# Cosine attention and a highway layer on one core: the order on each engine is handed from a manual schedule to the tile scheduler

## The chip, the cores and the metric

The kernel runs on one core of one Trainium2 chip. A core has five engines that each take instructions from a queue of their own: TensorE (PE, matrix products; its weight loads are listed apart as PEld), VectorE (DVE), ScalarE (ACT), GpSimd (POOL) and SyncE (SP), which here issues nearly all DMA transfers. [...] The metric is the device time of one execution in microseconds (us); lower is better.

## The reference

The work is a cosine-similarity attention over 8 batches with 12 heads of 448 positions and 64 dimensions, and behind it a highway layer on the 3584 x 768 result:

```python
q_n = q / (norm(q) + 1e-6);  k_n = k / (norm(k) + 1e-6)
scores = q_n @ k_n.T / tau                     # tau = 0.1
attn = exp(scores - max); attn /= sum(attn)
x = (attn @ v), heads side by side              # 3584 x 768
H = max(x @ w_h, 0);  T = sigmoid(x @ w_t + b_t)
out = T * H + (1 - T) * x
```

## The kernel before

**Tiles.** Four heads of one batch make a quad; there are 24 quads, three for each batch. The 448 positions are cut into a main part of 384 and a tail of 64; with its tails packed in pairs a quad is seven chunk-steps (`ci` 0 to 6). A step is one pair of score products on PE into a PSUM tile `sp` of two banks (line 258 for `ci` 0, line 266 for the others), one exponential on ACT of 128 x 896 into the tile `e` (line 279), and a share of the products of `e` with v (`av_slot`, line 295) into a PSUM tile `u` (main) or `ut` (tail). When a `u` is complete, DVE takes the reciprocal of the row sums (`rd`, line 319) and scales into `x` (line 321); a `ut` likewise (lines 343 and 344) into `xtail`.

**Preparing a quad.** `load_qk` brings q and k (line 91, and two short transfers each at line 100) into one of six `raw` buffers. ACT squares q (`sqq`, line 141), POOL squares k (`sqk`, line 147), DVE sums the squares (line 151) and makes the inverse root with integer and multiply steps (`rsqrt`, lines 158 to 170). POOL scales q and k (`qn` and `kn`, lines 182 to 211), and two transposing DMAs on SP (`turn`, lines 220 and 226) make `qT` and `kT`. DVE casts v (`vm` and `vt`, lines 236 and 243). The weights come in twelve transfers (line 123) through three `wst` buffers, and DVE casts each (line 127); the bias comes as `bt_raw` (line 464) and is halved on DVE into `bth` (line 465).

**The highway layer.** When the three quads of a batch are done, `ffn_items` queues its three row tiles of 128 (and for every second batch one tile of tails). A tile is six transposes on PE into `xp` (line 363), one copy on DVE into `xT` (line 365), and four groups of six products `pt` (line 381), two with w_t, which also get a bias product (line 394) and a tanh on ACT (`tt`, line 398), and two with w_h, which DVE turns into `hm` (line 386), `th` (line 407) and `o` (line 411). The result `o` goes out by SP (lines 419 and 425). A pool of two PSUM buffers holds `xp` and `pt`, another of two holds `u` and `ut`, a third of two holds `sp`.

**What sets the order.** The end of the kernel function emits everything step by step: the score product of the next step, the exponential of this one, a share of the av products, a ration of highway items (`RATE` 4.6 a step, taken from the queue `ffq`), and the preparing work that `prep` lists for this step. Line 68, `ctx.enter_context(tc.manual_schedule())`, binds this: inside the region each engine issues its instructions in the order in which they were emitted. The semaphores, and the buffers that the pools hand out, are worked out from that order.

Of the kernel before, what the change touches and what calls it, by code (L numbers as in the profile page):

```python
# [20 lines left out]
def kernel(  # L21
# [43 lines left out]
    u_ps = pool("u_ps", 2, space=PS)  # L65
    p_ps = pool("p_ps", 2, space=PS)

    ctx.enter_context(tc.manual_schedule())

    ident = const.tile([128, 128], FP16)  # L70
    w_h_f = const.tile([128, CC, DM], FP16)
# [536 lines left out]
```

## Time and profile before

| | |
|---|---|
| median of 2 runs | 468.95 us (466.25 and 471.65) |
| the profiled execution | 467.99 us, of which the span is 466.2 |
| busy: PE, DVE, ACT, POOL | 295.5, 275.6, 189.8, 156.2 us |
| mean granted TensorE clock | 0.87 |
| DMA moved | 61.03 MB, 131 GB/s |

No engine is busy for more than 63% of the span, so the idle time of PE, the busiest, and what ended it, is the thing to look at. The span has three parts that are read apart: the start, up to the first score product of quad 4 at 105.28 us, in which inputs and weights come in; the middle, from there to the first transposes of the last batch's highway tiles at 431.14 us, in which attention and highway layer run side by side; and the end, where four highway tiles are left.

### The profile page before, as it was taken

To read this page: it belongs to the slowest core of one execution; us is meant where nothing else is said; L and a number is where in the kernel's file an instruction comes from. 1 tells how busy PE (TensorE), PEld (TensorE's weight loads), DVE (VectorE), ACT (ScalarE), POOL (GpSimd) and SP (SyncE) were. 2 spreads that over 40 slices of the span, in tenths; PEclk is the share of its full clock that TensorE was granted. 3 is DMA by queue.
4 is the path that set the end of the run, shared out by engine and by line. 5 is a ranking of instruction groups with operands and counts; after the bars stand their busy time and mean duration, and the time that the engine had idled before them with its cause. 6 is when DMAs were issued, how large, how long until landed. Compare 5 with 4: busy or idle time off the path is not lost.

```text
span 466.2 us, 7225 instructions
## 1 busy us (share of the span) xinstructions
PE 295.5 (63%) x2768; PEld 157.3 (34%) x2768; DVE 275.6 (59%) x589; ACT 189.8 (41%) x249; POOL 156.2 (34%) x196
## 2 busy tenths in 40 slices
PE   0114051475784687775787688785588668888673
PEld 0002030232441344442343344343244334445342
DVE  3902996636762654685356777765456555555553
ACT  1224052343462554444345455552455235664110
POOL 2541742634253065136054436342530830000000
PEclk9999997668996988895758999989588879999989
DMA  9669599842935475553855294469353332200102
GB/s 243 154 149 268 146 268 269 191 105 67 250 47 141 128 190 126 134 101 90 221 124 141 82 251 101 104 150 219 95 97 77 77 77 65 48 36 35 67 34 67
DMA packets 111460, 61.03 MB, mean 131 GB/s; under 512 B 69441, under 2 KB 106305, under 8 KB 111426
## 3 DMA queue, kind: packets, MB, share of 16 engines
q1 hardware_dynamic: 110610, 60.12, 51.7%
q10 hardware_dynamic: 816, 0.46, 0.3%
q8 instruction: 21, 0.34, 0.3%
q14 instruction: 13, 0.11, 0.1%
HBM read 37.75 MB, written 11.01 MB: 105 GB/s over the span
## 4 chain that ended last, share of the span: by engine, by line
PE 37%; DVE 32%; SPq 9%; DMA 8%; POOL 5%; ACT 4%; issue 4%; DVEq 0%; ACTq 0%; POOLq 0%
PE pt L381 21%; PE u L295 7%; PE sp L266 6%; DVE o L411 6%; DMA raw<-in_q_dram 6%; DVE th L407 5%; DVE hm L386 4%; DVE n L151 4%; SPq L100 3%; DVE xT L365 3%; DVE x L321 3%; SPq L226 2%; ACT sqq L141 2%; ACT e L279 2%; PE pt L394 2%
## 5 line engine op out<-in xcount | busy, mean ns | idle before, releaser
L279 ACT ACTIVATE e<-sp 128x896 f16<-128x896 f32 x168 | 146.1, 917 | 45.3 <-PE sp L266 30.1
L381 PE MATMUL pt<-w_t_f,xT 128*128 128x384 f16 x336 | 86.2, 376 | 66.2 <-DVE xT L365 66.2
L266 PE MATMUL sp<-qT,kT 64*128 64x448 f16 x288 | 61.8, 424 | 58.4 <-ACT e L279 58.2
L381 PEld LDWEIGHTS <-xT 128*128 128x128 f16 x672 | 61.8, 106 | 108.9 <-DVE xT L365 71.1
L398 ACT ACTIVATE tt<-pt 128x384 f16<-128x384 f32 x56 | 27.5, 491 | 144.4 <-PE pt L394 144.4
L147 POOL TENSOR_TENSOR sqk<-raw 128x896 f16<-128x896 f32 x24 | 41.7, 1737 | 133.1 <-DMA raw<-in_k_dram 114.4
L295 PEld LDWEIGHTS <-e 128*128 128x128 f16 x1536 | 66.5, 106 | 53.3 <-issue 49.1
L381 PE MATMUL pt<-w_h_f,xT 128*128 128x384 f16 x336 | 80.3, 354 | 0.0
L182 POOL TENSOR_TENSOR qn<-raw,rs 128x384 f16<-128x384 f32 x46 | 41.0, 911 | 81.0 <-DVE rs L170 41.8
L295 PE MATMUL u<-vm,e 128*128 128x65 f16 x864 | 56.8, 209 | 17.2 <-DVE x L321 17.2
L319 DVE RECIPROCAL rd<-u 128x6 f32<-128x6 f32 x48 | 9.3, 193 | 84.2 <-PE u L295 84.2
L141 ACT ACTIVATE sqq<-raw 128x896 f16<-128x896 f32 x24 | 22.8, 948 | 73.4 <-DMA raw<-in_q_dram 65.8
L266 PEld LDWEIGHTS <-kT 64*128 64x128 f16 x288 | 15.9, 95 | 107.1 <-issue 102.4
L295 PE MATMUL u<-vt,e 128*128 128x65 f16 x288 | 48.8, 207 | 0.0
L386 DVE SCALAR_TENSOR_TENSOR hm<-pt,x 128x384 f16<-128x384 f32 x48 | 26.6, 554 | 37.3 <-PE pt L381 36.8
L202 POOL TENSOR_TENSOR kn<-raw,rs 128x384 f16<-128x384 f32 x48 | 42.7, 910 | 4.7 <-DVE rs L170 4.7
L407 DVE SCALAR_TENSOR_TENSOR th<-tt,hm 128x384 f16<-128x384 f16 x56 | 33.4, 596 | 5.8
L411 DVE SCALAR_TENSOR_TENSOR o<-x,th 128x384 f32<-128x384 f16 x48 | 30.0, 624 | 1.7
L151 DVE TENSOR_REDUCE n<-sqq 128x14 f32<-128x896 f16 x24 | 25.8, 1075 | 5.7 <-ACT sqq L141 5.6
L321 DVE SCALAR_TENSOR_TENSOR x<-u,rd 128x384 f16<-128x384 f32 x48 | 26.8, 557 | 1.6
L258 PE MATMUL sp<-qT,kT 128*128 128x448 f16 x48 | 15.0, 398 | 20.0 <-DMA kT<-kn 20.0
L151 DVE TENSOR_REDUCE n<-sqk 128x14 f32<-128x896 f16 x24 | 25.8, 1075 | 0.0
(43 smaller groups left out, 245.4 us busy)
## 6 DMA issues: line engine op xcount, KB each, us to landing
raw<-in_q_dram SPq DMA_DIRECT2D x24, 384.0 KB, 4.1
vr<-in_v_dram SPq DMA_DIRECT2D x8, 1152.0 KB, 7.2
out_dram<-o SPq DMA_DIRECT2D x24, 384.0 KB, 2.5
raw<-in_k_dram SPq DMA_DIRECT2D x23, 384.0 KB, 4.1
wst<-in_moe_w_h_dram SPq DMA_DIRECT2D x6, 384.0 KB, 5.4
wst<-in_moe_w_t_dram SPq DMA_DIRECT2D x6, 384.0 KB, 5.0
raw<-in_q_dram SPq DMA_DIRECT2D x48, 32.0 KB, 3.6
vtr<-in_v_dram SPq DMA_DIRECT2D x16, 96.0 KB, 6.7
```

The lines of the kernel that those rows point to most:

```text
L147: nc.gpsimd.tensor_mul(sq[:, :, :], rk, rk)
L151: nc.vector.reduce_sum(n2[:, qd, 14 * t : 14 * t + 14], st.pop((("sqq", "sqk")[t], Q))[:, :, :], axis=AX.X)
L182: eng.tensor_mul(qn[:, 4 * i : 4 * i + 3, :].rearrange("p j (h d) -> p h j d", h=2), raw[:, 6 * i : 6 * i + 6].rearrange("p (h j) d -> p h ...
L202: eng.tensor_mul(kn[:, 3 * i : 3 * i + 3, :].rearrange("p j (h d) -> p h j d", h=2), raw[:, g : g + 6].rearrange("p (h j) d -> p h j d", h=2),
L266: nc.tensor.matmul(sp[:, h, 0:S], lhsT=kT[hp, ci - 1, :], rhs=qT[hp, s * S : (s + 1) * S], start=True, stop=True,)
L279: nc.scalar.activation(st["e", Q][:, o : o + 2 * S].rearrange("p (a n) -> p a n", a=2), st.pop(("sp", g))[:, :, 0:S], AF.Exp, scale=inv_tau,)
L295: nc.tensor.matmul(u[:, slot, :], lhsT=e[:, o : o + 128], rhs=rhs, start=(kc == 0), stop=(kc == 3),)
L321: nc.vector.scalar_tensor_tensor(out=x[:, :, h0 : h0 + 2, :], in0=u[:, :, 0:D].rearrange("p (t h) d -> p t h d", h=2), scalar=0.0, in1=rd[ ...
L381: nc.tensor.matmul(loc["pt"][:, :], lhsT=loc["xT"][:, cc, :], rhs=w_f[:, cc, ms], start=(cc == 0), stop=(cc == CC - 1 and w_i == 0),)
L386: nc.vector.scalar_tensor_tensor(out=loc["hm"][:, ms], in0=loc["pt"][:, :], scalar=0.0, in1=xf[:, ms], op0=ALU.max, op1=ALU.subtract,)
L407: nc.vector.scalar_tensor_tensor(out=th[:, :], in0=loc["tt"][:, ms], scalar=1.0, in1=loc["hm"][:, ms], op0=ALU.add, op1=ALU.mult,)
L411: nc.vector.scalar_tensor_tensor(out=loc["o"][:, ms], in0=xf[:, ms], scalar=2.0, in1=th[:, :], op0=ALU.mult, op1=ALU.add,)
```

## The change

Line 68 is taken out. There is no other edit: every instruction, operand, buffer count and the emission are the same.

```diff
-    ctx.enter_context(tc.manual_schedule())
+
```

Without the region the tile scheduler sets the order while the program is built. It walks along a clock of its own with an estimated duration for every instruction and transfer. Whenever an engine comes free on that clock, it is given, of the instructions whose inputs and buffers are ready by then, the one that was emitted first. So the emission order stays as the priority, and an instruction is passed by later ones only while the scheduler holds it to be waiting. The order that comes out is fixed in the program; on the chip each engine still takes its queue from the front.

All 7225 instructions are there in both kernels. In the last tenth of PE's queue nothing changes place. On SP three transfers pass a neighbour before quad 14, and more behind it. Three places matter below. Numbers at the end of a name tell one buffer's uses apart; the numbers of the changed kernel are lower by two for the same thing (`u_592` before is `u_590` now).

The first place is DVE's queue in the start, around the bias (`bth`) and the first weight casts. In the kernel before, they stand after quad 1's v casts and ahead of the sums of quad 2 (`sqq_271`, `sqk_273`), with quad 0's first scaling (`x`) further behind:

```order
L236 CAST vm1_115<-vr_127 128x12x64
L243 CAST vt1_118<-vtr_128 64x2x64 x2
L465 TENSOR_SCALAR bth_108<-bt_raw_109 1x768
L151 TENSOR_REDUCE n2_172<-sqq_271 128x14
L151 TENSOR_REDUCE n2_172<-sqk_273 128x14
L158 TENSOR_SCALAR rs_173<-n2_172 128x28
```

In the changed kernel, DVE's queue has them here, right behind the scaling of quad 1's second half (`u_590`):

```order
L319 RECIPROCAL rd_631<-u_590 128x6
L236 CAST vm1_113<-vr_241 128x12x64
L321 SCALAR_TENSOR_TENSOR x_359<-u_590,rd_631 128x3x128
L243 CAST vt0_115<-vtr_242 64x2x64
L243 CAST vt1_116<-vtr_242 64x2x64 x2
L465 TENSOR_SCALAR bth_106<-bt_raw_107 1x768
L127 CAST w_h_f_104<-wst_248 128x768
L127 CAST w_h_f_104<-wst_250 128x768
```

The bias and the casts moved back past the sums of quads 2 to 4 and past all scalings of quads 0 and 1. The casts free the `wst` buffers, and SP's queue, which did not change there, has the fourth weight transfer ahead of quad 2's transposes.

The second place is one highway tile of the middle (`xp_1684` before, `xp_1682` now; weight loads and repeats left out). On PE before, the first product group follows the transposes at once, and the next step's scores come behind its first two products:

```order
L295 MATMUL ut_1669<-vt1_118,e_1493 128x65
L363 MATMUL xp_1684<-ident_105,x_863 128x128
L381 MATMUL pt_1696<-w_t_f_107,xT_1691 128x384
L266 MATMUL sp_1699<-qT_1377,kT_1419 128x448
L295 MATMUL ut_1669<-vm1_115,e_1493 128x65
```

On PE in the changed kernel, two score products, eight av products and one half of the next scores stand between:

```order
L363 MATMUL xp_1682<-ident_103,x_861 128x128
L266 MATMUL sp_1697<-qT_1375,kT_1417 128x448
L295 MATMUL ut_1667<-vm1_113,e_1491 128x65
L295 MATMUL ut_1667<-vt1_116,e_1491 128x65
L266 MATMUL sp_1723<-qT_1375,kT_1417 128x448
L381 MATMUL pt_1694<-w_t_f_105,xT_1689 128x384
```

On DVE, the copy that these products wait for (`xT`) stood before behind the tile ahead's `hm`, `th` and `o`:

```order
L386 SCALAR_TENSOR_TENSOR hm_1515<-pt_1627,x_863 128x384
L407 SCALAR_TENSOR_TENSOR th_1680<-tt_1516,hm_1515 128x384
L411 SCALAR_TENSOR_TENSOR o_1517<-x_863,th_1680 128x384
L365 COPY xT_1691<-xp_1684 128x768
L343 RECIPROCAL rdt_1712<-ut_1669 64x4
```

and now stands on DVE right behind `hm`:

```order
L386 SCALAR_TENSOR_TENSOR hm_1513<-pt_1625,x_861 128x384
L365 COPY xT_1689<-xp_1682 128x768
L407 SCALAR_TENSOR_TENSOR th_1678<-tt_1514,hm_1513 128x384
L343 RECIPROCAL rdt_1710<-ut_1667 64x4
L411 SCALAR_TENSOR_TENSOR o_1515<-x_861,th_1678 128x384
```

So the copy moved ahead of two operations on DVE, and its reader moved back past a step of attention on PE. Counted over all 28 tiles, 21 had nothing between their transposes and their first product group before; in the changed kernel only the four tiles of the end have nothing between. There the copy still moves ahead of `th` and `o`.

The third place is ACT's queue in quads 2 and 3, and in it the squares of a later quad's q. Before, the squares of quad 7 (`raw_540`) stand behind the third exponential of quad 2 (`e_569`), and those of quad 8 (`raw_697`) behind the first of quad 3 (`e_722`):

```order
L141 ACTIVATE sqq_636<-raw_540 128x896
L279 ACTIVATE e_569<-sp_617 128x896
L279 ACTIVATE e_569<-sp_643 128x896
L279 ACTIVATE e_569<-sp_653 128x896
L279 ACTIVATE e_569<-sp_675 128x896
L279 ACTIVATE e_722<-sp_705 128x896
L141 ACTIVATE sqq_735<-raw_697 128x896
```

In the changed kernel, the squares of quad 7 stand on ACT behind the fourth exponential of quad 3 (`e_720`), and those of quad 8 behind the first of quad 4 (`e_915`):

```order
L279 ACTIVATE e_720<-sp_756 128x896
L141 ACTIVATE sqq_634<-raw_538 128x896
L279 ACTIVATE e_720<-sp_802 128x896
L279 ACTIVATE e_720<-sp_815 128x896
L279 ACTIVATE e_720<-sp_845 128x896
L398 ACTIVATE tt_785<-pt_787 128x384
L398 ACTIVATE tt_785<-pt_837 128x384
L279 ACTIVATE e_915<-sp_881 128x896
L141 ACTIVATE sqq_733<-raw_695 128x896
```

They moved back by eight and by seven exponentials. The squares of quad 6 moved from behind the third exponential of quad 1 to behind its last; those of quad 3 from behind quad 0's third exponential to behind its fourth. Those of quads 10 and 11 moved back by seven, those of quads 12 to 17 by none to four, and from quad 18 on they moved forward, with their loads on SP.

## The prediction

> **What bounds the kernel now.** I read the page first, for an engine that could be the bound by its work alone, then the busy time of PE in the three parts of the span, then what PE waited for in each part, and last the stretches that carry a wait.
>
> ```profile
> span 466.2 us, 7225 instructions
> ...
> PE 295.5 (63%) x2768; PEld 157.3 (34%) x2768; DVE 275.6 (59%) x589; ACT 189.8 (41%) x249; POOL 156.2 (34%) x196
> ...
> L279 ACT ACTIVATE e<-sp 128x896 f16<-128x896 f32 x168 | 146.1, 917 | 45.3 <-PE sp L266 30.1
> ...
> L319 DVE RECIPROCAL rd<-u 128x6 f32<-128x6 f32 x48 | 9.3, 193 | 84.2 <-PE u L295 84.2
> ```
>
> No engine is full. The windows of PE (length, busy time and count, granted clock, DMA share, GB/s) put the start, the middle and the end side by side:
>
> ```profile
> 0.00:105.28 105.28, 32.42 (x299) 0.89 0.79 199
> 105.28:431.14 325.86, 242.21 (x2343) 0.86 0.48 117
> 431.14:466.20 35.06, 20.88 (x130) 0.92 0.16 56
> ```
>
> The waits of PE alone (total, times, longest), first of the start, then of the middle, then of the end:
>
> ```profile
> PE sp L266 <- ACT e L279: 34.7, 8, 9.9
> PE sp L258 <- DMA kT<-kn: 20.0, 1, 20.0
> PE u L295 <- DVE x L321: 17.2, 1, 17.2
> ...
> PE pt L381 <- DVE xT L365: 57.5, 23, 5.1
> PE sp L266 <- ACT e L279: 23.6, 12, 6.6
> PE xp L363 <- DVE x L321: 2.3, 3, 1.5
> ...
> PE pt L381 <- DVE xT L365: 8.1, 4, 2.0
> ```
>
> In the middle the account closes: 242.2 busy and 57.5 + 23.6 + 2.3 = 83.4 waiting make 325.6 of 325.9 us. So the middle is PE's work plus three waits, 20 quads at 16.3 us each. The largest wait is for the copy `xT`, 2.5 us each time. The busy time holds a loss of its own, which single quads show (columns: length; PE, PEld, DVE, ACT and POOL busy; clock; DMA):
>
> ```profile
> 136.50:156.40 19.90, 12.09 (x107) 6.22 (x106) 8.36 (x18) 7.06 (x10) 4.01 (x5) 0.74 0.53 135
> 274.60:286.50 11.90, 10.26 (x120) 5.83 (x119) 8.90 (x17) 8.36 (x12) 5.76 (x7) 1.00 0.63 149
> 389.70:402.00 12.30, 10.26 (x121) 5.84 (x119) 6.59 (x17) 7.58 (x11) 0.00 (x0) 1.00 0.31 74
> ```
>
> The same amount of products takes 12.1 us at a clock of 0.74 and 10.26 at 1.00. The middle's mean is 12.1 a quad, so at most 20 x 1.85 = 37 us of it is slow clock. The two fast quads, at 11.9 and 12.3 us, show how short a quad gets when the waits stay away.
>
> **The start, term A.** The timeline, in order of time (start, length, engine, line, what; in brackets the idle time before and what ended it):
>
> ```profile
> 3.58 2.82 SPq L114 DMA_DIRECT2D vtr<-in_v_dram  x2
> 11.80 0.19 DVE L169 TENSOR_TENSOR ta<-ta,rs 128x28 f32<-128x28 f32 x1
> 12.03 0.19 DVE L170 SCALAR_TENSOR_TENSOR rs<-ta,rs 128x28 f32<-128x28 f32 x1
> 12.91 1.66 DVE L182 TENSOR_TENSOR qn<-raw,rs 128x384 f16<-128x384 f32 x2
> 20.03 0.93 PE L258 MATMUL sp<-qT,kT 128*128 128x448 f16 x2 [20.03 <-DMA kT<-kn]
> 32.96 0.95 ACT L141 ACTIVATE sqq<-raw 128x896 f16<-128x896 f32 x1 [8.59 <-DMA raw<-in_q_dram]
> 36.63 0.92 ACT L279 ACTIVATE e<-sp 128x896 f16<-128x896 f32 x1 [0.30 <-PE sp L266]
> 38.14 0.92 ACT L279 ACTIVATE e<-sp 128x896 f16<-128x896 f32 x1 [0.60 <-PE sp L258]
> 42.95 0.55 DVE L465 TENSOR_SCALAR bth<-bt_raw 1x768 f16<-1x768 f32 x1 [18.88 <-DMA bt_raw<-in_moe_b_t_dram]
> 53.75 0.55 DVE L127 CAST w_h_f<-wst 128x768 f16<-128x768 f32 x1
> 62.61 0.95 ACT L141 ACTIVATE sqq<-raw 128x896 f16<-128x896 f32 x1 [15.52 <-DMA raw<-in_q_dram]
> 66.82 0.94 PE L258 MATMUL sp<-qT,kT 128*128 128x448 f16 x2
> 79.72 0.95 ACT L141 ACTIVATE sqq<-raw 128x896 f16<-128x896 f32 x1 [8.49 <-DMA raw<-in_q_dram]
> 81.90 0.35 SPq L123 DMA_DIRECT2D wst<-in_moe_w_t_dram  x1
> 83.92 0.94 PE L258 MATMUL sp<-qT,kT 128*128 128x448 f16 x2
> 87.55 1.76 DVE L127 CAST w_t_f<-wst 128x768 f16<-128x768 f32 x2
> 105.28 0.54 PE L258 MATMUL sp<-qT,kT 128*128 128x448 f16 x2
> ...
> DMA to landing us min/median/max: 5.8/6.7/9.3
> ```
>
> The last row is of `vtr`. The first edit is a loss: DVE now has the v casts ahead of and among quad 0's inverse root. The second tail transfer is issued near 5.0 and lands 5.8 to 9.3 later, at 10.8 to 14.3, with 3.6 us still to come: eight root steps and six tail casts of 0.22 us (the distance of the rows at 11.80 and 12.03) and a cast of 0.55 like the one at 53.75. So `qn`, begun at 12.91, begins at 14.4 to 17.9, and the first product comes 1.5 to 5 us later; I take 4, at 24.
>
> Quad 3's squares still stand in front of an exponential of quad 0, and their load is still behind quad 1's transposes on SP, so that wait ends some 3 us later than at 32.96 too, and the exponentials go on at about 37. Ten are then left in quads 0 and 1. The rows at 36.63 and 38.14 give 1.51 us for a step, so quad 1 is through at 37 + 15 = 52 and its last `x` at about 55. Three stalls that held quad 1 before are gone: `bth` no longer stands in front, the squares of quad 6 (15.52 us of waiting) come behind its last exponential, and `x` of quad 0 doesn't wait 17.2 us.
>
> This gain is given back at once. The weight casts now stand behind that last `x`, so they begin at 55 instead of 53.75, and SP has the fourth weight transfer, which needs a freed buffer, ahead of quad 2's transposes. Quad 2 therefore starts at 68, where it was 66.82; PE idles 13 us. What stays is behind it. Quad 2 ran into the squares of quad 7 (8.49 us); these now come in quad 3, so its seven steps take 10.6 us and quad 3 starts at 78.5, not 83.92. Quad 3 waits for the last w_t weights: their transfer was issued at 81.90 and cast by 89.3, and stands now behind the last `x` of quad 2 (about 80) and one more cast, so it comes 0 to 2 us later, and PE finishes the two product groups that need it and starts quad 4 at about 92. Term A is 92 - 105.28 = -13. Its bounds are -16 (quad 3 at 1.51 us a step from 78.5, weights no later) and +3 (the weights later by a transfer of about 5 us at each of three places where SP waits for a cast).
>
> **The middle, term B.** The copy `xT`: its DVE place is priced by the end of the run, where nothing else is between.
>
> ```profile
> 432.05 0.56 DVE L407 SCALAR_TENSOR_TENSOR th<-tt,hm 128x384 f16<-128x384 f16 x1
> 432.64 0.56 DVE L411 SCALAR_TENSOR_TENSOR o<-x,th 128x384 f32<-128x384 f16 x1
> 433.12 0.55 DVE L365 COPY xT<-xp 128x768 f16<-128x768 f16 x1
> 440.50 1.15 PE L381 MATMUL pt<-w_t_f,xT 128*128 128x384 f16 x6 [2.04 <-DVE xT L365]
> 447.28 2.10 PE L381 MATMUL pt<-w_t_f,xT 128*128 128x384 f16 x6 [2.04 <-DVE xT L365]
> ```
>
> Ahead of `th` and `o` it starts 433.12 - 432.05 = 1.07 us sooner. On PE, the 24 tiles outside the end now have on average four score products, two steps, between transposes and first group, against half a product before; two steps are at least 2 x 0.917 = 1.8 us of ACT's pace. 2.5 - 1.07 - 1.8 is below nothing, but seven tiles have one step between, so I leave 0.5 us a tile, 12 us: -45. The bounds are -57 and -25 (1.07 alone).
>
> The waits for `e` in the middle (23.6 us) come from squares that wait for their load in front of an exponential. The squares move back by seven exponentials for quads 10 and 11, by four or fewer up to 17, forward behind: I take half, -12.
>
> A cost is new. Steps that were padded with highway products now run bare, about 40 of them more (95 score products between, in pairs, against 14 before). A bare step goes at ACT's pace: at least 0.92, and 1.51 us as it was at 36.63, against some 0.64 us of PE's work at full clock: of a fast quad's 10.26 us, 28/24 tiles of 26 products at 1.15/6 = 0.19 us (row at 440.50) are 5.8, and the rest goes to seven steps. That is 0.28 to 0.87 us a step, 11 to 35 us; I take 18.
>
> Waits: -45 - 12 + 18 = -39. With fewer long waits the clock recovers. Equal waits of 2.04 us at 440.50 and 447.28 were followed by six products in 1.15 and in 2.10 us, so even a short wait can cost the clock; I take 10 of the 37 us. [...] B is -39 - 10 = -49, bounds -84 (below) and 0. B makes 13.8 us a quad, between the 12 of the fast quads and the 16.3 of now.
>
> DVE's 275.6 us are 69% of a span of 400, so its work alone doesn't bind. POOL, the loads and the transposes are covered as before: a quad's transposes are emitted one and a half quads ahead of their use, some 20 us at the new pace.
>
> **The end, term C.** PE's order is the same and the copy starts 1.07 us sooner in four tiles: -4.
>
> **Sum.** 466.2 - 13 - 49 - 4 = 400, and 1.8 outside the span (467.99 - 466.2) make 402 us. The profiled execution lies 1.0 below the median of the runs shown, which is left out.
>
> **Rivals.**
>
> *The waits only change their name* (20%). DVE takes its queue in order, and some `hm`, which wait for product groups that now come late, stand in front of a `rd` and `x` that free a `u` buffer for PE. For it speaks that DVE already waited for PE's `u` 84.2 us and that both wait for each other; against it, that `x` passed `th` and `o` in many places too. At 1.5 us in each of 24 tiles, 36 us come back: B is -13 and the time 438.
>
> *Nothing is left* (8%). An order built on estimated durations blocks where the chip is slower, as the order by hand did at `bth`, 18.88 us for one transfer. With B at 0 and A at +3 the time is 467. [...]
>
> *Slower, through the weights* (5%). The casts behind quad 1's last `x` hold three buffers, these the fourth weight, this SP's queue and with it all later transposes. Every microsecond that this `x` comes after 55 moves quad 4. From 68 on the start gains nothing. If the v load of batch 1 or the sums of quads 3 and 4, which stand ahead of that `x`, hold it until 86, A is +18; with B at 0 the time is 482. Against it speaks that their loads are issued where they were, and quad 1 would have to end 31 us later than reckoned.
>
> *Better* (5%): all 20 quads as the fast ones, 12.1 us: B is -84, the time 367.
>
> **How the numbers follow.** The forecast has 62%, and 378 to 430 as its own range, from B between -73 and -25, and up to 4 us on top for A. The range of 376 to 442 takes in the forecast and the first rival, and leaves out the other three. Two percent of 468.95, about what two runs that lie 1.2% apart can tell from no change, are 9.4 us: faster is the forecast, the first and the last rival, 87%; the same is 8%, slower 5%.
>
> **What would show it.** In the changed kernel's profile, PE's wait for `xT` should be below 20 us in the middle and some 4 at the end; quad 4 should start near 92, quad 2 near 68 after a wait of some 13 us for `kT`; the wait for `bth` should be gone; the middle's clock should be above 0.88. I am wrong if quad 4 starts after 105, or if PE waits more than 30 us for `x` of line 321, or over 50 for `e`, in the middle.

## The result and the profile after

The changed kernel takes 379.75 us (median of 377.95 and 381.54) against 468.95 us: a ratio of 0.810, 95% interval 0.784 to 0.836, which is 368 to 392 us. Times in this document are medians of all runs of a kernel, while ratios and intervals leave out runs more than 1.5% above its fastest. The change is faster, below the 402 us of the prediction, inside its range of 376 to 442 and close to its lower end.

The page of the changed kernel, span, engines and the row of the exponentials:

```profile
span 375.9 us, 7229 instructions
...
PE 274.6 (73%) x2768; PEld 153.8 (41%) x2768; DVE 271.6 (72%) x589; ACT 194.9 (52%) x249; POOL 157.7 (42%) x196
...
L279 ACT ACTIVATE e<-sp 128x896 f16<-128x896 f32 x168 | 149.4, 917 | 61.5 <-PE sp L266 37.7
```

The page counts four instructions more than before; the counts of the five engine rows are the same. PE needs 21 us less for its 2768 products. The same three parts, cut at the first score product of quad 4 and at the first transposes of the last batch's tiles (length, PE busy and count, granted clock, DMA share, GB/s):

```profile
0.00:89.13 89.13, 35.31 (x338) 0.81 0.85 220
89.13:347.52 258.39, 220.05 (x2304) 0.94 0.65 153
347.52:375.90 28.38, 19.23 (x130) 0.96 0.19 69
```

The 0.81 of the start, and the 0.89 before, can't be read as a clock. From 22 to 35 us the profile gives 1.00, yet a pair of score products of line 266 takes 0.56 us there (at 22.88), as it does at a clock of 0.50 (at 95.97), against 0.36 at 1.00 (at 90.62).

The start is 16.2 us shorter, the middle 67.5, the end 6.7; together 90.3 us of the profiled execution (466.2 to 375.9). What PE waits for (total, times, longest), in the start, then the middle, then the end:

```profile
PE sp L258 <- DMA kT<-kn: 35.1, 2, 22.0
PE sp L266 <- ACT e L279: 8.0, 6, 5.8
...
PE pt L381 <- DVE xT L365: 13.3, 8, 3.7
PE u L295 <- DVE x L321: 7.1, 3, 3.2
PE sp L266 <- ACT e L279: 5.7, 6, 4.0
PE xp L363 <- ACT tt L398: 3.9, 1, 3.9
PE xp L363 <- DVE x L321: 3.0, 3, 1.4
PE pt L381 <- DVE hm L386: 2.9, 3, 1.1
PE u L295 <- DVE xtail L344: 1.6, 2, 0.8
...
PE pt L381 <- DVE xT L365: 3.0, 4, 0.8
```

In the middle 13.3 us are left of 57.5 for `xT`, and 6 (with one more wait of 0.3) of 23.6 for `e`. Five small waits are new or larger: for `x`, `xtail`, `hm` and `tt`, 18.5 us where 2.3 stood for `x`. The waits fell from 83.4 to 37.8 us, PE's busy time from 242.2 to 220.05.

The start in order of time (start, length, engine, line, what):

```profile
22.02 0.93 PE L258 MATMUL sp<-qT,kT 128*128 128x448 f16 x2 [22.02 <-DMA kT<-kn]
32.43 0.95 ACT L141 ACTIVATE sqq<-raw 128x896 f16<-128x896 f32 x1 [6.10 <-DMA raw<-in_q_dram]
51.51 0.55 DVE L321 SCALAR_TENSOR_TENSOR x<-u,rd 128x384 f16<-128x384 f32 x1
52.90 0.55 DVE L465 TENSOR_SCALAR bth<-bt_raw 1x768 f16<-1x768 f32 x1
53.38 1.48 DVE L127 CAST w_h_f<-wst 128x768 f16<-128x768 f32 x3
65.52 0.93 PE L258 MATMUL sp<-qT,kT 128*128 128x448 f16 x2 [13.12 <-DMA kT<-kn]
76.39 0.84 PE L258 MATMUL sp<-qT,kT 128*128 128x448 f16 x2
89.13 0.54 PE L258 MATMUL sp<-qT,kT 128*128 128x448 f16 x2
```

The bias no longer carries a wait, quad 1 is scaled at 51.5, PE then stands idle for 13 us until quad 2's keys are there, and quads 3 and 4 follow without a long stall.

### The profile page after: what moved, and what is told of

Same layout as the page of the kernel before. It is cut to its first block, busy times and chain, and to the rows that moved or that the text cites. A ratio compares the mean times of both kernels' runs of the same rounds, so it can differ in the third digit from the quotient of the medians.

```text
span 375.9 us, 7229 instructions
## 1 busy us (share of the span) xinstructions
PE 274.6 (73%) x2768; PEld 153.8 (41%) x2768; DVE 271.6 (72%) x589; ACT 194.9 (52%) x249; POOL 157.7 (42%) x196
## 4 chain that ended last, share of the span: by engine, by line
PE 34%; DVE 27%; POOL 15%; issue 8%; DMA 8%; SPq 4%; ACT 3%; POOLq 0%; ACTq 0%; DVEq 0%
PE pt L381 19%; DVE n L151 6%; PE u L295 5%; PE sp L266 5%; POOL kn L202 4%; DMA raw<-in_q_dram 4%; POOL qn L182 4%; POOL sqk L147 4%; DVE hm L386 3%; DVE o L411 3%; DMA raw<-in_k_dram 2%; DVE vt L243 2%; POOL kn L211 2%; DVE x L321 2%; SPq L100 2%
## 5 line engine op out<-in xcount | busy, mean ns | idle before, releaser
L279 ACT ACTIVATE e<-sp 128x896 f16<-128x896 f32 x168 | 149.4, 917 | 61.5 <-PE sp L266 37.7
L381 PE MATMUL pt<-w_t_f,xT 128*128 128x384 f16 x336 | 76.6, 353 | 18.4 <-DVE xT L365 16.4
L295 PEld LDWEIGHTS <-e 128*128 128x128 f16 x1536 | 64.0, 102 | 45.9 <-issue 31.8
L381 PE MATMUL pt<-w_h_f,xT 128*128 128x384 f16 x336 | 73.6, 335 | 3.1 <-DVE hm L386 2.9
L266 PE MATMUL sp<-qT,kT 64*128 64x448 f16 x288 | 58.6, 388 | 14.0 <-ACT e L279 13.6
L295 PE MATMUL u<-vm,e 128*128 128x65 f16 x864 | 55.7, 202 | 12.6 <-DVE x L321 9.0
L295 PE MATMUL u<-vt,e 128*128 128x65 f16 x288 | 45.8, 199 | 0.0
L407 DVE SCALAR_TENSOR_TENSOR th<-tt,hm 128x384 f16<-128x384 f16 x56 | 38.2, 682 | 2.0 <-ACT tt L398 0.2
L151 DVE TENSOR_REDUCE n<-sqq 128x14 f32<-128x896 f16 x24 | 25.8, 1079 | 18.1 <-ACT sqq L141 18.1
L411 DVE SCALAR_TENSOR_TENSOR o<-x,th 128x384 f32<-128x384 f16 x48 | 34.9, 726 | 0.9
L243 DVE CAST vt<-vtr 64x128 f16<-64x128 f32 x48 | 18.5, 385 | 8.0 <-PE u L295 7.4
```

Source lines behind the costliest of these rows:

```text
L151: nc.vector.reduce_sum(n2[:, qd, 14 * t : 14 * t + 14], st.pop((("sqq", "sqk")[t], Q))[:, :, :], axis=AX.X)
L266: nc.tensor.matmul(sp[:, h, 0:S], lhsT=kT[hp, ci - 1, :], rhs=qT[hp, s * S : (s + 1) * S], start=True, stop=True,)
L279: nc.scalar.activation(st["e", Q][:, o : o + 2 * S].rearrange("p (a n) -> p a n", a=2), st.pop(("sp", g))[:, :, 0:S], AF.Exp, scale=inv_tau,)
L295: nc.tensor.matmul(u[:, slot, :], lhsT=e[:, o : o + 128], rhs=rhs, start=(kc == 0), stop=(kc == 3),)
L381: nc.tensor.matmul(loc["pt"][:, :], lhsT=loc["xT"][:, cc, :], rhs=w_f[:, cc, ms], start=(cc == 0), stop=(cc == CC - 1 and w_i == 0),)
L407: nc.vector.scalar_tensor_tensor(out=th[:, :], in0=loc["tt"][:, ms], scalar=1.0, in1=loc["hm"][:, ms], op0=ALU.add, op1=ALU.mult,)
```

## The experiments

Two theories were to be told apart. Mine: the gain is the sum of few stalls, each made by two engines' places in a row: the highway tile (PE's order and the copy's place on DVE), the squares in front of exponentials (ACT), and the bias (DVE). The rival: the gain needs all engines in a common order, so that no part of it can be had alone. The line numbers of a kernel with an engine held or freed are higher by one.

### One engine held in the order of emission, the others scheduled

```diff
-    ctx.enter_context(tc.manual_schedule())
+    E = mybir.EngineType
+    ctx.enter_context(tc.manual_schedule(engines={E.PE}))
```

and the same with DVE, with Activation (ACT), and with SP and Pool.

> PE keeps the emission order, the scheduler orders the other four engines. If the gain of the middle needs both places (the copy ahead of th and o on DVE, and attention work between transposes and first group on PE), PE's wait for xT goes back up from 16 us to about 35 (1.07 us off each of the 57.5 + 8.1 us before, in 28 tiles), the clock falls with it, and the time is 400 to 415 us; the start stays near 89 us. If DVE's order alone earned the gain, the time stays below 388 us.

> DVE keeps the emission order, the other four engines are scheduled. By the account of the start, the wait for bth (18.88 us before) comes back and with it x of quad 0 and the end of quad 1; the first quad-4 product is at 95 to 105 us instead of 89. The end gets back about 5 us. In the middle the copy is 1.07 us later, partly covered: 5 to 15 us. In all 400 to 415 us. If DVE's order alone earned the gain, 450 us or more; if PE's alone, below 388.

> ACT keeps the emission order, the other four are scheduled. If the place of the squares matters as reckoned, the stalls of quads 2 and 3 (8.49 and 6.90 us of waiting for a load) are back and quad 4 starts near 100 us, and PE's wait for e in the middle goes from 6 back to about 20 us: 395 to 412 us. If only PE and DVE matter, below 385.

> SP and POOL keep the emission order, PE, DVE and ACT are scheduled. SP's queue hardly changed before quad 14 and POOL is never waited for by PE, so by the account 375 to 385 us. If the order of loads and transposes carried part of the gain, above 390.

| held | time, us | ratio to before (95%) | quad 4 starts, us |
|---|---|---|---|
| none (the change) | 379.75 | 0.810 (0.784 to 0.836) | 89.1 |
| PE | 404.58 | 0.862 (0.846 to 0.877) | 92.9 |
| DVE | 391.63 | none, runs of 386.7 and 396.6 | 88.9 |
| ACT | 380.94 | 0.811 (0.808 to 0.814) | 95.9 |
| SP and POOL | 385.69 | 0.821 (0.813 to 0.830) | 90.0 |

With PE held, PE's wait for `xT` over the whole run is 43.0 us in 25 times (35 expected), against 16.4 in the change: PE's order was worth 25 us, and the mechanism is the expected one. With DVE held the faster run lies 7 us above the change and the other, which is the profiled one, 17; 400 to 415 us were expected, a miss. The wait behind the bias returned in the start, 18.1 us of PE for `x`:

```profile
PE sp L259 <- DMA kT<-kn: 22.8, 3, 20.0
PE pt L382 <- DVE xT L366: 21.7, 16, 3.7
PE u L296 <- DVE x L322: 20.9, 7, 18.1
```

Yet quad 4 starts at 88.9, as in the change, where I had expected 95 to 105. The wait for `x` stands in the place of the 13 us for quad 2's keys, which are gone. So the bias, the third of my stalls, cost the start nothing here; in the profiled run the end has 6.8 us more than in the change, the middle the rest.

With DVE's faster run, the four losses sum to 39 of 89 us, and only the one with PE held lies outside the interval of the change; SP and POOL ended 0.7 us above the 375 to 385 expected. ACT alone was a plain miss in time: I had expected 395 to 412 us, because the squares stand in front of exponentials again. Half of that came true. The start is 6.8 us longer (PE waits 31.2 us for `e` there, against 8.0), but the middle is 3.0 us shorter, with 3.2 us of waits for `e`, so hardly anything was lost in all.

### One engine scheduled, the others held

The set of held engines is now all but PE, and then all but DVE.

> Only PE is ordered by the scheduler, the other four keep the emission order. If PE's order earns its part of the middle by itself, xT's wait drops from 66 us to about 25 (1.8 us of cover in 24 tiles), the clock gives 10 back, and the start and the end stay as before: 412 to 430 us. If PE's order were nearly the whole gain, as its 25 us of loss when held suggests against 1 to 12 for the others, 385 to 400 us. If it needs the other engines to follow, above 445.

> Only DVE is ordered by the scheduler. The copy is 1.07 us sooner in 28 tiles (30 us), bth and the casts no longer stand in front in the start, but ACT's squares of quads 6, 7 and 8 still do, so quad 4 starts at 98 to 105: 425 to 442 us. If DVE's order matters little by itself, above 455.

PE alone: 422.63 us (0.902, 0.888 to 0.917), as expected, though quad 4 starts at 100.2, 5 us sooner than before. DVE alone: 457.83 us (0.977, 0.966 to 0.989), a miss, and a gain of 2.3% that is hardly clear of the noise. What PE waits for with DVE alone scheduled:

```profile
PE sp L267 <- ACT e L280: 88.2, 22, 16.6
PE pt L382 <- DVE xT L366: 36.7, 24, 4.9
```

The wait for `xT` over the whole run fell by 29.5 us (66.2 to 36.7), and the wait for `e` rose by 30 (58.2 to 88.2): the saved time was handed to the next wait. So what one engine's order saves is not a term that can be added to the others.

### The stalls taken away by hand

The kernel before with its order by hand, and two edits: the last `th` and `o` of a tile are emitted behind the next tile's copy, and a step's ration of highway items ends at the transposes, so that the first product group comes a step later.

```diff
-                        fin(ms, mh)
+                        if mh == 1:
+                            late.append((fin, ms, mh))
+                        else:
+                            fin(ms, mh)
...
+            if c == 2.0 and not last:
+                break
```

The list `late` is emptied behind the next copy. A second kernel adds to this the squares of far quads (from quad 6 on) four steps later, with their sums on DVE two to four steps later, and a third has this move alone:

```diff
-            put(at, sq_q, R)
+            put(min(at + 4, 6), sq_q, R)
             put(2, sq_k, R)
-            put(at + 2, red, R, 0)
             put(5, red, R, 1)
+            put(6, red, R, 0)
```

> Every engine keeps an emission order, but by hand: the last th and o of a tile are emitted behind the next tile's copy xT, and a step's highway ration ends after the transposes, so that the first product group comes one step later. Nothing else moves. If the wait for xT is the cause in the middle, it falls from 57.5 to below 15 us there, the clock recovers 5 to 15 us, bare steps cost some 10: 410 to 428 us, with quad 4 still at 105. If the scheduler's other moves earned the middle, above 440.

> As the hand-made tile order, and the squares of q of a quad to come are emitted four steps later on ACT (and their sums two to four steps later on DVE). If the squares in front of an exponential cost the 23.6 us of waits for e and the start its 8.49 and 6.90 us, the time falls by 12 to 28 us below the hand-made tile order alone. If ACT's place doesn't matter, as holding ACT in emission order cost 1 us, by less than 6.

> The kernel before, with only the squares of far quads emitted four steps later (as in the hand-written pair, without its copy and product edits). On top of those two edits the squares were worth 33 us. If the waits for e and for xT are separate, they are worth about as much alone: 430 to 442 us, PE's wait for e falls from 58 us to under 20, and its wait for xT stays at 55 to 75 us. Rival: the waits for xT, which are left, absorb the gain (PE then waits there for longer): 450 to 464 us, with PE's wait for xT over 80 us.

| edit | time, us | ratio (95%) | PE's wait for `xT` | for `e` (line 266) |
|---|---|---|---|---|
| none (before) | 468.95 | | 66.2 | 58.2 |
| tile | 431.0 | 0.920 (0.909 to 0.931) | 18.1 | 80.0 |
| squares | 441.41 | 0.937 (0.931 to 0.944) | 70.3 | 11.9 |
| both | 398.1 | 0.850 (0.840 to 0.859) | 32.1 | 12.3 |

The times of one row's kernel and of before are from the same chip in each ratio. The waits are those of the whole run. The tile edit is worth 8.0%, the squares 6.3%, both 15.0%, as much as the two together within the noise. Two sizes were missed: the tile edit ended 3 us above the 410 to 428 expected, and on top of it the squares brought 33 us where 12 to 28 were expected. Two stalls thus make some 70 of the 89 us, and each can be had alone, by a few lines and without a scheduler. That speaks for my theory over the rival, with the reservations that a part of the tile's gain is paid out as waits for `e` (58 to 80) until the squares move too, and that the bias has no part in it that a run shows. Of the remaining 19 us of the span, 11 are in the start: quad 4 begins at 100.12 here and at 89.13 in the change. What makes these 11 was not taken apart.

### Why ACT's order alone costs next to nothing

Squares in front of exponentials cost 6% in the order by hand, and next to nothing where only ACT is held. With ACT held, SP's queue turned out to have loads of q and k earlier from quad 12 on: that of quad 23's q, for one, passes six transposing DMAs, those of three quads. So I held SP as well.

> ACT and SP are both held in the order of emission; PE, DVE and POOL are scheduled. With ACT alone held the time was 380.9 us, and SP's queue then had the loads of q and k up to three transposes earlier than before (from the twelfth quad on). Theory: the squares' place on ACT costs nothing only because SP brings their loads earlier. With SP's order back, the squares wait for their loads in the middle again (in the middle none did with ACT alone held), PE's wait for e in the middle is over 20 us, and the time is 395 to 412 us. Rival: the squares' place and SP's order are each worth what they cost alone, 1 and 6 us; then the time is 383 to 390 us and PE waits under 10 us for e in the middle.

It takes 400.09 us (0.842, 0.833 to 0.852), 19 more than with ACT alone held, and 16 more by its two faster runs (394.85 and 399.36). The waits of ACT from quad 4 on, first with ACT held, all that are listed, then the two largest with ACT and SP held, then PE's wait for `e` behind quad 4 in the two kernels, in the same order:

```profile
ACT tt L399 <- PE pt L395: 103.1, 53, 7.8
ACT e L280 <- PE sp L267: 14.6, 6, 5.9
ACT e L280 <- PE sp L259: 3.6, 4, 2.6
ACT sqq L142 <- DVE rdt L344: 0.5, 1, 0.5
```

```profile
ACT tt L399 <- PE pt L395: 68.3, 41, 5.5
ACT sqq L142 <- DMA raw<-in_q_dram: 58.2, 11, 15.7
```

```profile
PE sp L267 <- ACT e L280: 3.2, 11, 0.7
```

```profile
PE sp L267 <- ACT e L280: 21.7, 19, 5.1
```

This settles it for the part behind the start. With ACT held and SP free, no square waits for its load from quad 4 on; with SP held too, they wait 58.2 us, PE waits 18.5 us more for `e`, and the middle takes 272.3 us instead of 255.4. Here a square that stood too early in ACT's queue was cured on ACT, by moving it back (with the squares edit alone PE's wait for `e` fell from 58.2 to 11.9 us), or on SP, by moving its load forward (58.2 us of the squares' waits to none). In the start SP's order cured nothing: the squares wait 37 us for loads there in both kernels.

### The 13 us before quad 2

The largest wait that is left after quad 0's is for quad 2's keys. The first edit on the changed kernel gives the raw weights six buffers, so that SP need not wait for a cast:

```diff
-    wst_p = pool("wst", 3)
+    wst_p = pool("wst", 6)
```

> The changed kernel with six buffers for raw weights where it has three; the order on every engine is the same. SP no longer waits from 49.8 to 53.95 us for a cast before it can go on to quad 2's transposes. Theory (the weight buffers hold the start): quad 2 starts near 58 us where it was 65.5, quad 4 near 82 where it was 89.1, and the time is 370 to 375 us. Rival (the transfers themselves, or the norms on POOL, set quad 2's keys): quad 2 starts at 62 or later, quad 4 at 86 or later, and the time is 377 to 381 us.

It takes 376.21 us (0.795, 0.787 to 0.802), which these runs can't tell from the change: quad 2 starts at 62.26 instead of 65.52, quad 4 at 87.67. The rival's starts hold, and the time lies 1 us below its range; SP's wait for the cast, 4.1 us, was worth 3.3 us of quad 2's start, and the rest of the 13 us lies elsewhere. The second edit also brings the first six weight loads forward, behind quad 0's transposes:

```diff
+        if Q == 0:
+            for i in range(6):
+                load_w(i)
...
-    for i in range(3):
-        load_w(i)
...
-                if j + 3 < 2 * CC:
-                    put(s_ + 3, load_w, j + 3)
+                if j + 6 < 2 * CC:
+                    put(s_ + 3, load_w, j + 6)
```

> The changed kernel with six weight buffers whose first six loads are emitted behind quad 0's transposes, so that SP issues them before quad 1's transposes, between 20 and 29 us, where the DMA engines were half idle (115 GB/s from 22 to 35 us, against 208 to 278 from 35 to 89). Theory (the transfers between 35 and 60 us hold quad 2's keys): 2.4 MB less is moved there, quad 2 starts at 54 to 59 us (62.3 with six buffers alone, 65.5 in the changed kernel), quad 4 at 79 to 84, and the time is 364 to 372 us. Rival (the norms on POOL and the order of SP set quad 2's keys, or the weight casts, which now stand among quad 1's root steps, hold quad 1 back): quad 2 starts at 61 or later and the time is 374 to 384 us.

It takes 365.12 us (0.781, 0.775 to 0.788). All four of its runs (364.62 to 368.85) lie more than 9 us below both of the changed kernel's, though the intervals of the two ratios just overlap (0.784 and 0.788). Windows of the changed kernel and then of this one (length; PE, PEld, DVE, ACT, POOL busy; clock; DMA share; GB/s):

```profile
22.00:35.00 13.00, 6.39 (x47) 3.02 (x48) 5.66 (x17) 5.91 (x8) 8.20 (x12) 1.00 0.48 115
50.00:65.00 15.00, 1.09 (x15) 0.69 (x12) 8.11 (x16) 1.79 (x2) 5.55 (x8) 0.50 0.81 208
```

```profile
22.00:35.00 13.00, 6.82 (x54) 3.28 (x54) 6.49 (x20) 5.88 (x7) 6.91 (x9) 1.00 0.99 280
50.00:65.00 15.00, 4.19 (x20) 1.31 (x21) 12.68 (x24) 5.84 (x8) 12.17 (x15) 1.00 1.05 274
```

The DMA engines' lull from 22 to 35 us is filled (115 to 280 GB/s). Quad 2 starts at 59.98, just later than expected, and still waits 10.9 us; quad 4 starts at 80.75. Of the 13.0 us that the span gets shorter, 8.4 are in the start and 4.6 in the middle.

My theory that the transfers hold quad 2's keys is not borne out: the load from 50 to 65 us did not fall (208 to 274 GB/s). What moved is the place of quad 2's key transpose in time on SP, in the change, with six buffers and with early weights:

```profile
60.75 1.27 SPq L226 DMA_TRANSPOSE kT<-kn  x1
57.41 1.28 SPq L226 DMA_TRANSPOSE kT<-kn  x1
55.11 1.26 SPq L226 DMA_TRANSPOSE kT<-kn  x1
```

Quad 2 starts 4.77, 4.85 and 4.87 us behind it. In the change, SP waits for the cast until 53.95 and then issues ten transfers one behind the other, until 60.75, before it comes to this one; POOL was done with the keys by 52.3. With early weights the like ten begin at 48.11, since three weight issues (3.7 us of SP) and the wait for the cast no longer stand ahead of them. So it is SP's queue of issues that holds quad 2's keys, more than the transfers' speed. What the earlier casts on DVE add behind quad 2 was not taken apart.

## Why the prediction was right, and where it was wrong

**Term A, the start: -16.2 against -13.** The chain was the predicted one, and every point of it came 1.6 to 3.5 us early: quad 1's last `x` at 51.5 (55), the weight casts at 53.4 (55), quad 2 at 65.5 after 13.1 us of waiting (68 after 13), quad 3 at 76.4 (78.5), quad 4 at 89.1 (92). Two steps were mis-sized. The v casts delay the first product by 2.0 us (20.03 to 22.02), within the bounds of 1.5 to 5, where I took 4. And quad 3's squares were through their wait at 32.43, before the 32.96 of the kernel before and not 3 us behind it. I had their load behind quad 1's transposes on SP; in fact SP issued its large transfer at 20.16 (28.07 before), ahead of these transposes (25.70), so the delay of quad 0 did not reach it.

**Term B, the middle: -67.5 against -49.** The waits I knew came out: `xT` -44.2 (I took -45) and `e` -17.6 (-12).

The cost of bare steps at ACT's pace was wrong in kind, and that its size came out near is luck. I took +18 us; new waits did come, +16.2, but they are small waits for buffers and inputs from DVE and ACT (`x`, `xtail`, `hm`, `tt`), and PE waits only 6 us for `e` in the middle. A quad with its highway products shows who sets the pace (columns as above):

```profile
302.60:312.60 10.00, 10.00 (x116) 5.77 (x115) 7.16 (x19) 7.45 (x10) 0.00 (x0) 1.00 0.55 89
```

PE is busy for all of it and ACT for three quarters. In the changed kernel ACT waits for `sp` of line 266 for 37.7 us, more than the 30.1 before: ACT follows PE. I had priced a step by 36.63 to 38.14 of the start, where PE and ACT take turns, and carried that over to a place where they don't.

The step that failed by size is the clock. I took 10 of 37 us. The middle's busy time fell by 22.2 us, of which about 4 are the 39 products that moved to the start (39 at 242.21/2343 = 0.103 us) and 18 are the clock, 0.86 to 0.94. The shorter waits explain it. My two rows for the price of a slow clock were no like pair, since they hold 107 and 120 products; the 37 us, from the middle's mean, don't rest on them. Six products with w_t after a wait for `xT` (the wait stands in the brackets), in the order of time in the changed kernel:

```profile
93.62 2.10 PE L381 MATMUL pt<-w_t_f,xT 128*128 128x384 f16 x6 [1.90 <-DVE xT L365]
107.45 2.10 PE L381 MATMUL pt<-w_t_f,xT 128*128 128x384 f16 x6 [2.86 <-DVE xT L365]
354.36 1.15 PE L381 MATMUL pt<-w_t_f,xT 128*128 128x384 f16 x6 [0.78 <-DVE xT L365]
```

After 0.78 us the group takes 1.15 us at a granted clock of 1.00, after 1.90 and 2.86 it takes 2.10 at 0.50. Before, the waits were 2.5 us on average, 23 of them in the middle; now eight are left. The 10 us were an estimate of mine that rested on the pair of rows at 440.50 and 447.28 alone. I should have asked how busy PE is left in each stretch of 3.41 us, the grid on which the traces show the clock to step (last section).

**Term C, the end: -6.7 against -4.** The copy runs ahead of `th` and `o` as foreseen:

```profile
353.76 0.55 DVE L365 COPY xT<-xp 128x768 f16<-128x768 f16 x1
354.22 0.55 DVE L407 SCALAR_TENSOR_TENSOR th<-tt,hm 128x384 f16<-128x384 f16 x1
```

The waits fell from 2.04 to 0.78 us each, 5 us in all (1.26 each, near the 1.07 that I took), and the group that took 2.10 us at 447.28, at a clock of 0.50, is gone: all four now take 1.15, the clock again.

**Sum.** A, B and C were short by 3.2, 18.5 and 2.7 us, 24.4 together; outside the span lie 2.05 us, not 1.8. Of this, some 8 us (B) and the one group of 2.10 us (C) are clock, 6.6 are the two known waits (`xT` and `e`, 4.8) and the new ones (1.8), and the rest of B's busy time is the products that I had not counted as moved to the start, about 4.

**The rivals.** *The waits only change their name* is refuted: PE's waits for `x` in the middle are 10.1 us, not 36. *Nothing is left* falls with the 67.5 us of the middle. *Slower, through the weights* falls with quad 1's `x` at 51.5, far from the 68 and 86 at which it would have begun to bite; that the weights' place on SP is a lever is shown by the 13 us of the early weights. *Better* (12.1 us a quad) came close: the middle is 12.9 us a quad.

**The marks** all held: `xT` below 20 us (13.3) in the middle and near 4 at the end (3.0), the bias without a wait, the middle's clock above 0.88 (0.94), quad 2 behind 13 us of waiting. What they could not show is that my reading of the parts as a sum was too simple: with one engine held, the loss was 25, 7 (DVE's faster run), 1 and 6 us, the wait behind the bias moved quad 4 by nothing, and the same squares cost 6% or next to nothing, depending on another engine's queue.

## What to carry to other kernels

Both traces have all 589 operations of DVE and all 248 activations of ACT in the order of the program, and an instruction that waited for a transfer held up what stood behind it: 18.88 us at `bth` on DVE, 15.52 at the squares of quad 6 on ACT. So the thing to change is its place, or its load's place on the queue that issues it; here either did, and a run with both held showed it. When PE's waits get shorter, price the clock too, by how busy PE is left in each stretch of the length in which the clock steps (3.41 us in these traces); here it brought 18 us beside 46 of waits. After a change that reorders everything, read the queue that issues the transfers ahead of the longest wait, and move loads that depend on nothing out of it, into a stretch where the DMA engines are half idle, as they were here from 22 to 35 us (a busy share of 0.48).

## What the runs showed of the hardware that was not expected

**In both traces the clock stepped on a grid of 3.41 us, by how busy PE had been in the stretch before.** Groups of w_t products ran at a clock of 0.50 after all six waits for `xT` of 3.6 us or more (at 163.76 before, from the second product on), and after some between 1.56 and 2.86, so the length of a wait alone doesn't decide. In the traces of both kernels, the times between two steps of the clock are whole multiples of 3.41 us. Stretches of that grid, each with the one behind it, first of the changed kernel and then of the kernel before (length; PE, PEld, DVE, ACT, POOL busy; clock; DMA share; GB/s):

```profile
90.18:93.59 3.41, 1.54 (x14) 0.63 (x11) 3.26 (x5) 2.96 (x4) 1.68 (x1) 1.00 1.26 150
93.59:97.00 3.41, 3.38 (x11) 1.25 (x12) 3.08 (x6) 0.93 (x2) 0.00 (x0) 0.50 1.06 302
437.01:440.42 3.41, 1.45 (x13) 0.89 (x11) 2.94 (x6) 0.49 (x1) 0.00 (x0) 1.00 0.00 0
440.42:443.84 3.42, 3.33 (x21) 2.04 (x22) 0.94 (x3) 0.49 (x1) 0.00 (x0) 1.00 0.29 115
```

Of the stretches at full clock in these two traces, from the first step on record, each of the 24 with PE busy for less than 40% was followed by half the clock, and none of the 115 with 60% or more; of the 19 between, four were. The way back took more: behind a stretch at half the clock, full clock came only where PE had been busy for 79.5% of it or more (83% once was not enough). By these counts a wait of 2.5 us costs the clock when it falls into one stretch, since it leaves PE at most 27% of it, and a shorter one did when another wait fell into the same: at 251.78 before, 0.65 us for `xT` followed 1.5 us for `x`, PE was busy for 1.24 of the 3.41 us, and the clock fell 0.9 us later. What decides between 40 and 60% is open.

**`th` and `o` on DVE got slower or faster with their place.** The rows of `th` and `o`, of the kernel before and then of the changed one (busy and mean ns behind the bar):

```profile
L407 DVE SCALAR_TENSOR_TENSOR th<-tt,hm 128x384 f16<-128x384 f16 x56 | 33.4, 596 | 5.8
L411 DVE SCALAR_TENSOR_TENSOR o<-x,th 128x384 f32<-128x384 f16 x48 | 30.0, 624 | 1.7
L411 DVE SCALAR_TENSOR_TENSOR o<-xtail,th 128x384 f32<-128x384 f16 x8 | 7.3, 913 | 0.3
```

```profile
L407 DVE SCALAR_TENSOR_TENSOR th<-tt,hm 128x384 f16<-128x384 f16 x56 | 38.2, 682 | 2.0 <-ACT tt L398 0.2
L411 DVE SCALAR_TENSOR_TENSOR o<-x,th 128x384 f32<-128x384 f16 x48 | 34.9, 726 | 0.9
L411 DVE SCALAR_TENSOR_TENSOR o<-xtail,th 128x384 f32<-128x384 f16 x8 | 4.5, 566 | 0.1
```

`th` and `o` from `x` take 14 to 16% longer, `o` from `xtail` 38% less, while `hm` (554 to 550 ns) and `xT` (550 to 547) stay. The change moves them only in time, and the traces show what they then run beside. In the two kernels, the 147 executions of `th` and `o` during which POOL did nothing took 0.53 to 0.56 us each; every longer one, up to 2.07 us, ran while POOL was busy. `hm` and `xT` take at most 0.56 us beside POOL too. Whether POOL's work is the cause, and why it would slow the one kind and not the other, no run shows.
